# Linear attention on query features turned by VectorE instead of TensorE, with some VectorE work on GpSimd

## The chip, the cores and the metric

The kernel runs on one core of a Trainium2 chip. A core has five engines that work side by side and wait for one another through semaphores: TensorE (PE in the profile; PEld is its loading of weights), VectorE (DVE), ScalarE (ACT), GpSimd (POOL) and SyncE (SP, which here only issues DMAs). The time is that of one execution on the device, in microseconds; less is better.

## The reference

Two branches work on the same normalised tokens x (S = 2048 tokens, D = 512), and their sum and x make the output. Cut to what matters:

```python
xn = layernorm(x)
# A: linear attention, H = 32 heads of Dh = 16, features by two softmaxes
q, k, v = split(xn @ wqkv)
phi_q = concat(softmax(q @ w_phi), softmax(-(q @ w_phi)))      # 32 features a head
phi_k = concat(softmax(k @ w_phi), softmax(-(k @ w_phi)))
kv  = einsum("bhsf,bhsd->bhfd", phi_k, v);  z = sum_s phi_k
o   = (phi_q @ kv) / (phi_q @ z + 1e-6)
A   = o @ wo
# B: gated MLP with a product over tokens, Fh = 688
u   = gelu(xn @ w_in);  z1, z2 = u[:, :Fh], layernorm(u[:, Fh:])
B   = (z1 * (w_sp @ z2 + b_sp)) @ w_out
out = x + A + B
```

## The kernel before

Tokens are cut into 16 tiles of 128 rows. All large products are made from split operands: a value is rounded to a high part (`round_h`, on ACT), the rest is taken by a subtraction (`rest_l`, on VectorE unless another engine is named), and `mm3` (L55 to L57) adds three TensorE products, high by high, high by low and low by high.

The work goes in stages. First, projections: for each tile the features of q and k before their last scaling are made and those of q are stored in DRAM (`e_d`, 1024 values a token and 64 reciprocals of the softmax sums), as is `z1`; k's are added into the key-value sums. From these come `kvT` (the key-value matrix of each head, 16 x 32) and `zb` (the key sums, one row of 1024 copied to every partition). The features of q of tiles 0 and 1 are finished here already and stored back. Then the second half of `w_in`, its layer norm, and the product over tokens (`g`, L55 to L57, until about 494 us), made with seven products in place of eight in blocks of two by two; VectorE prepares its operands (`prep_a`, L537 to L541) and ACT and VectorE round them (L47, L51). The gated rows go through DRAM and come back turned (`uT`, `ut`).

The last stage makes the output, tile by tile. For a tile:

- `q_fin` (L494 to L501) finishes the q features on VectorE: weigh the 1024 features by `zb` (L494), sum them by head (L495), form the scale of each head (L496 to L499), scale the features (L501).
- `attend_T` (L896, L898) turns the features of two tiles on TensorE, sixteen transposes of 128 x 128, and ACT copies them out of PSUM (L900).
- `attend` (L912) multiplies the turned features of two tiles with `kvT`: sixteen products, each on a 64-row by 32-column part of the array, 256 columns (two tiles) long. ACT rounds the result and VectorE takes the rest (`oT`).
- `gated` joins the turned gate (L774, ACT), rounds it (`uh`, ACT) and takes the rest (`ul`, L51, VectorE).
- `project_u` multiplies it with `w_out` (17 products of 512 columns, `pout<-wu`, with L933), `project_o` adds the attention with `wo` (12 products, `pout<-woh`), VectorE adds x (`xr`, L944) and SP stores the rows.

The order on an engine is that of the program where the text puts instructions behind others with `tc.issue_after`; a planner orders the rest. In the last stage a pair of tiles goes `project_u`, `attend`, `project_u`, two `project_o`, `attend_T` of the next pair. Features are finished three tiles ahead. From tile 6 on, POOL copies finished features to another tile by a DMA (`er<-et`, L872), so that the transposes can read them in the faster type.

SP's queue is served in order: loads of `et` (from `e_d`), of `ut` and of `xr`, and the stores of the output, which wait for L944.

Of the kernel before, what the change touches and what calls it, by code (L numbers as in the profile page):

```python
# [19 lines left out]
P = 128  # L20
S, D, H, DH, FH = 2048, 512, 32, 16, 688
NT = S // P
# [17 lines left out]
def mixer(ctx: ExitStack, tc: tile.TileContext, x, x_t, wv, wqkT, phi_bd, wo, w_in, wst, b_r, w_out, out):  # L40
# [449 lines left out]
    def q_fin(et, tmp, zb):  # L490
# [3 lines left out]
        dve.tensor_tensor(tmp, e, zb, op=ALU.mult)  # L494
# [6 lines left out]
        return e, dve.tensor_tensor(heads(e), heads(e), bc(w, 2 * H), op=ALU.mult).ins  # L501
# [46 lines left out]
    with ExitStack() as p1:  # L548
# [41 lines left out]
        for s in range(NE):  # L590
            et = load_q(s, tb.tile([P, QW], F32, tag="et", bufs=2, name="et"))
            tmp = zw.tile([P, 4, FC], F32, tag="z2", bufs=2, name="qtmp").rearrange("p a b -> p (a b)")[:, :NF]
            e, _ = q_fin(et, tmp, zb)
            sp.dma_start(e_d[s, :, :NF], e)
# [131 lines left out]
    def gate(i, cb, z, planes):  # L726
# [9 lines left out]
        dve.tensor_copy(z[:, :, rm], rh.bitcast(F32))  # L736
        planes = planes.bitcast(U16).rearrange("p (k two n) -> p k two n", k=2, two=2)
        for k in range(2):
            act.activation(planes[:, k], halves(z[:, k]), AF.Copy)
# [12 lines left out]
    def split_w(t, h, l):  # L752
        return round_h(act, h, t), rest_l(l, t, h)
# [23 lines left out]
    def gate_parts(u, h, l, rt):  # L777
        full = slice(0, KF * P)
        round_h(act, h, u[:, full])
        lasts[1] = rest_l(l, u[:, full], h)  # L780
# [6 lines left out]
    def first_gate(t, rt):  # L787
        b = slot("uh_ul", F32R)
        u = xz2.tile([P, 2, 2, FC], F32, tag="b", name="u0").rearrange("p a b c -> p (a b c)")[:, :UP]
        return gate_parts(joined(t, u), b[:, :KF * P], b[:, KF * P:2 * KF * P], rt)  # L790

    lasts, wu = [None] * 6, []

    def first_q(s):
        e = slot("eq", F32R)[:, :NF]
        sp.dma_start(e.bitcast(F32), e_d[s, :, :NF])
        return e
# [12 lines left out]
    g, es, ets = {}, {}, {}  # L810
    for n in range(NC):
# [16 lines left out]
        if n == NC - 3:  # L828
            zs = slot("zb", F32R)
            zb, ident_r = zs[:, :NF].bitcast(F32), zs[:, NF:NF + P]  # L830
            round_h(act, ident_r, ident)
# [4 lines left out]
            q2 = slot("qtmp")[:, :NF]  # L836
        if n == NC - 2:
            u1t = load_u(1, slot("u1").bitcast(U16)[:, :2 * UP])
            es[0], es[1] = first_q(0), first_q(1)
            ets[3] = load_q(3, slot("et"))  # L840
            wo_raw = []
            for c in range(ND):
                rows = [(r, r + QP) for r in range((c % 2 * NG * 2 + c // 2) * QP, D, 2 * QP)][:NG]
                t = ws.tile([P, QC, P], F32, tag=f"f{c // 2}", bufs=2, name="wof").rearrange("p a b -> p (a b)")
                with tc.issue_after(load_q.last):
                    wo_raw.append(load_part((sp, pool)[c % 2], wo, rows, t))
    cb = drain(NP - 1, g, slot("c").rearrange("p (a b) -> p a b", a=4))
    with tc.issue_after(cb[1]), tc.issue_after(cb[2]):
        uT.append(first_gate(u1t, wu_rest[1]))
    with tc.issue_after(lasts[1]):  # L850
        es[2], last = q_fin(ets.pop(2), q2, zb)
    mid.close()

# [5 lines left out]
    fin = []  # L859
# [176 lines left out]
```

## Time and profile before

| what | value |
|---|---|
| median of 3 runs | 629.76 us (629.31 to 629.93) |
| profiled execution, first to last instruction | 628.4 us |
| PE busy | 622.3 us (99%) |
| VectorE busy | 505.3 us (80%) |
| ScalarE busy | 313.5 us (50%) |
| GpSimd busy | 121.0 us (19%) |
| DMA, mean over the span | 180 GB/s |

The profiled execution is one run under the profiler; the time of a run holds about 1.4 us outside this span. A busy PE is not a PE at its peak: products are pipelined, a product's row of 0.39 us stands for some 0.23 us of the chain.

Rows of a group give line, engine, operation, result and operands with their shapes, the count, then the busy time in us, the mean of one in ns, and the idle time of the engine before them with what ended it. Rows of a timeline or of the chain begin with start and duration in us. Rows of a windows view give a stretch, its length, the busy time of PE, PEld, DVE, ACT and POOL in it, the clock granted to TensorE, the share of the DMA engines and GB/s. Rows of one line's instructions give the shortest, median and longest duration in ns.

### The profile page before, as it was taken

Reading aid. Unit: us, or ns where it says so; the run is one execution under the profiler, and the core shown is the slowest. Engines: PE = TensorE matmul, PEld = TensorE weight load, DVE = VectorE, ACT = ScalarE, POOL = GpSimd, SP = SyncE. Lnnn points to the kernel's source line nnn. Section 1 sums busy time; section 2 is a strip of 40 time slices with the busy share of each in tenths; the row PEclk is TensorE's granted clock in tenths of the full one; section 3 lists DMA queues with packets and bytes.
Section 4 is the critical chain, followed back from the end, with each engine's and each line's share of the span. In section 5 each row is a group of like instructions: output and inputs, shape, how many; then the busy total and the mean of one; then the engine's idle time right before and its main releaser. Section 6 shows DMA issues by size and latency. Waiting matters only on the chain.

```text
span 628.4 us, 11487 instructions
## 1 busy us (share of the span) xinstructions
PE 622.3 (99%) x4375; PEld 563.1 (90%) x4375; DVE 505.3 (80%) x925; ACT 313.5 (50%) x463; POOL 121.0 (19%) x213
## 2 busy tenths in 40 slices
PE   9999999999999999999999999999999999999997
PEld 6888888888888999999999999999999878877776
DVE  5979989998988579989987677786777789989721
ACT  5623333432343447788553654546445655557550
POOL 4552232222101004552010110101101200110100
PEclk9999999999999999999999999999999999999999
DMA  8467767555653861001467758667588966897921
GB/s 326 152 160 163 200 176 162 166 157 151 165 164 106 265 211 68 2 1 57 138 173 186 221 176 203 202 184 226 165 197 297 287 227 230 268 278 263 293 83 35
DMA packets 67091, 112.85 MB, mean 180 GB/s; under 512 B 30588, under 2 KB 32124, under 8 KB 67036
## 3 DMA queue, kind: packets, MB, share of 16 engines
q1 hardware_dynamic: 53036, 63.35, 34.8%
q0 software_dynamic: 11408, 42.61, 23.8%
q10 hardware_dynamic: 2592, 6.16, 2.6%
q8 instruction: 34, 0.56, 0.4%
q14 instruction: 21, 0.17, 0.1%
HBM read 60.69 MB, written 31.48 MB: 147 GB/s over the span
## 4 chain that ended last, share of the span: by engine, by line
PE 96%; DVE 3%; issue 0%; ACT 0%
PE g L57 11%; PE g L56 11%; PE g L55 11%; PE proj L55 6%; PE zps L55 6%; PE proj L57 6%; PE proj L56 6%; PE zps L57 6%; PE zps L56 6%; PE pout L55 6%; PE pout L56 5%; PE pout L57 5%; PE po L912 1%; PE kvps L322 1%; PE ptq L898 1%; PE pout L933 1%
## 5 line engine op out<-in xcount | busy, mean ns | idle before, releaser
L55 PE MATMUL g<-B,A 128*128 128x344 f32 x448 | 143.2, 320 | 0.0
L56 PE MATMUL g<-B,A 128*128 128x344 f32 x448 | 143.2, 320 | 0.0
L57 PE MATMUL g<-B,A 128*128 128x344 f32 x448 | 143.0, 320 | 0.0
L57 PEld LDWEIGHTS g<-B,A 128*128 128x128 f32 x448 | 84.1, 188 | 0.2 <-DVE A L51 0.2
L56 PEld LDWEIGHTS g<-B,A 128*128 128x128 f32 x448 | 84.2, 188 | 0.0
L55 PEld LDWEIGHTS g<-B,A 128*128 128x128 f32 x448 | 84.2, 188 | 0.0
L47 ACT ACTIVATE A<-S 128x512 fp32r<-128x512 f32 x64 | 39.4, 628 | 63.3 <-DVE S L538 40.4
L116 ACT ACTIVATE e<-e,r_x 128x1024 f32<-128x1024 f32 x32 | 36.7, 1148 | 46.0 <-DVE e L115 44.1
L51 DVE TENSOR_TENSOR A<-S,A 128x512 fp32r<-128x512 f32 x64 | 43.1, 684 | 9.7 <-ACT A L47 9.6
L55 PE MATMUL proj<-wqk_h,xT 128*128 128x512 f32 x124 | 49.6, 400 | 0.0
L57 PE MATMUL proj<-wqk_h,xT 128*128 128x512 f32 x124 | 48.8, 394 | 0.0
L56 PE MATMUL proj<-wqk_l,xT 128*128 128x512 f32 x124 | 48.7, 393 | 0.0
L118 DVE TENSOR_REDUCE sm<-e 128x64 f32<-128x1024 f32 x32 | 38.6, 1210 | 9.7 <-ACT e L116 9.5
L47 ACT ACTIVATE A<-wf 128x512 fp32r<-128x512 f32 x64 | 33.0, 516 | 19.4 <-PE g L57 8.7
L51 DVE TENSOR_TENSOR A<-wf,A 128x512 fp32r<-128x512 f32 x64 | 35.2, 549 | 9.2 <-ACT A L47 9.0
L55 PE MATMUL zps<-w_h,xT 128*128 128x344 f32 x128 | 41.8, 326 | 0.4 <-ACT z1f L146 0.3
L57 PE MATMUL zps<-w_h,xT 128*128 128x344 f32 x128 | 40.9, 319 | 0.0
L56 PE MATMUL zps<-w_l,xT 128*128 128x344 f32 x128 | 40.8, 319 | 0.0
L537 DVE TENSOR_TENSOR S<-wf 128x256 f32<-128x256 f32 x32 | 13.4, 420 | 27.1 <-DMA wf<-in_wst 27.1
L146 ACT ACTIVATE z1f<-zps,r_x 128x344 f32<-128x344 f32 (+1 forms) x30 | 17.0, 565 | 33.8 <-PE zps L57 33.3
L302 ACT ACTIVATE v<-proj,r_x 128x512 f32<-128x512 f32 x16 | 11.0, 685 | 44.2 <-PE proj L57 41.7
L900 ACT ACTIVATE f<-ptq 128x512 f32<-128x512 f32 x32 | 16.5, 604 | 26.7 <-PE ptq L898 16.8
(199 smaller groups left out, 1546.4 us busy)
## 6 DMA issues: line engine op xcount, KB each, us to landing
wf<-in_wst SPq DMA_DIRECT2D x64, 256.0 KB, 3.9
e_d<-e POOLq DMA_DIRECT2D x16, 544.0 KB, 3.7
et<-e_d SPq DMA_DIRECT2D x16, 544.0 KB, 5.5
zacc<-e POOLq DMA_DIRECT2D x16, 512.0 KB, 4.9
z_d<-z1f ACTq DMA_DIRECT2D x16, 344.0 KB, 3.8
z1t<-z_d POOLq DMA_DIRECT2D x16, 344.0 KB, 5.8
u_d<-c POOLq DMA_DIRECT2D x14, 384.0 KB, 2.7
er<-et POOLq DMA_DIRECT2D x10, 512.0 KB, 4.9
```

Of the source, the lines that this page charges most:

```text
L47: return act.activation(h, src, AF.Copy).ins
L51: return (eng or dve).tensor_tensor(l, src, h.bitcast(F32), op=ALU.subtract).ins
L55: pe.matmul(dst, ah, bh, start=start, stop=False)
L56: pe.matmul(dst, ah, bl, start=False, stop=False)
L57: return pe.matmul(dst, al, bh, start=False, stop=stop).ins
L116: softmax_pair.exp = act.activation(e, e, AF.Exp, scale=scale).ins
L118: dve.tensor_reduce(sm, heads(e), axis=AX.X, op=ALU.add)
L146: z1_raw.last = act.activation(z[:, k], p, AF.Copy, scale=r_x[:, s:s + 1]).ins
L302: ins = act.activation(v[s], proj(s, wv_h, wv_l, rest_last), AF.Copy, scale=r_x[:, s:s + 1]).ins
L322: ins = pe.matmul(kv_acc[k:k + QP, m // 4], vs[:, m * QP:(m + 1) * QP], e[:, m * HP:(m + 1) * HP], start=s == 0 and m < 4, stop=s == NT - ...
L537: dve.tensor_tensor(sums[:, 0], b[:, 0], b[:, 1], op=ALU.add)
L900: attend_T.last = act.activation(f, pt.rearrange("p a k b -> p a (k b)"), AF.Copy).ins
```

## The change

Query features. `q_fin` no longer weighs; a function of its own does it, on an engine that is named, and `q_fin` ends with a transpose on VectorE in blocks of 32 x 32: within each block of 32 tokens and one head's 32 features, features come to lie on the partitions. Tiles 0 and 1 are stored turned. The transposes on TensorE, the copies out of PSUM and POOL's copies of finished features are gone.

Attention. Four copies of the key-value matrix (`kv4`), one for each 32 partitions, replace `kvT`. One run takes four token tiles: 64 products, each on a 32 x 32 part of the array and 128 columns long (32 tokens of each of four tiles); the order takes first the two upper strips of 32 rows, then the two lower ones. There are four runs instead of eight.

Engines. GpSimd takes the weighing of tiles 2 to 15, the rests of the gate for tiles 1 to 15, and the rests of `w_out` and `wo`. Two early weighings and the rest of gate 0 stay on VectorE.

Order. The last stage is written out by hand: every step stands behind the last instruction of the same engine (`in_line`). PSUM buffers for the output go from three to four, those for the rest from five to four. `wo` is loaded in four DMAs instead of sixteen.

The core of the diff:

```diff
+    def q_weigh(et, tmp, zb, eng):
+        return eng.tensor_tensor(tmp, et[:, :NF], zb, op=ALU.mult).ins
+
-    def q_fin(et, tmp, zb):
+    def q_fin(et, tmp, eT):
...
-        dve.tensor_tensor(tmp, e, zb, op=ALU.mult)
         dve.tensor_reduce(t, heads(tmp), axis=AX.X, op=ALU.add)
...
-        return e, dve.tensor_tensor(heads(e), heads(e), bc(w, 2 * H), op=ALU.mult).ins
+        dve.tensor_tensor(heads(e), heads(e), bc(w, 2 * H), op=ALU.mult)
+        return dve.transpose(eT, e).ins
...
     def split_w(t, h, l):
-        return round_h(act, h, t), rest_l(l, t, h)
+        return round_h(act, h, t), rest_l(l, t, h, pool)
...
-    def gate_parts(u, h, l, rt):
+    def gate_parts(u, h, l, rt, eng=None):
         full = slice(0, KF * P)
         round_h(act, h, u[:, full])
-        lasts[1] = rest_l(l, u[:, full], h)
+        lasts[1] = rest_l(l, u[:, full], h, eng)
...
+    def weigh(s):
+        tmps[s] = slot("qtmp")[:, :NF]
+        line["pool"] = q_weigh(ets[s], tmps[s], zb, pool)
...
+            kv4 = slot("kv4")[:, :4 * 2 * NG * QP].rearrange("p (r j b) -> p r j b", r=4, j=2 * NG)
+            for i in range(P // SQ):
+                sp.dma_start(kv4[i * SQ:(i + 1) * SQ].rearrange("p r j b -> p r (j b)"),
+                             kvT_d.rearrange("(r f) x -> f r x", f=SQ))
+            weigh(2)
...
+    with tc.issue_after(cb[1]), tc.issue_after(line["pool"]):
+        uT.append(first_gate(u1t, wu_rest[1], pool))
...
+    pso = ctx.enter_context(psum("pso", 4))
+    pst = ctx.enter_context(psum("pst", 4))
...
+    def features(s):
+        with in_line():
+            line["dve"] = q_fin(ets.pop(s), tmps.pop(s), turned(s))
...
+    def attend(k):
+        eg = egs.pop(k)
+        oT = [cw.tile([P, NG, QT, P], F32R, tag=f"oT{n}", bufs=1, name="oT") for n in "hl"]
+        po = [pst.tile([P, NG, QT, SQ], F32, tag="po", name="po") for _ in range(P // SQ)]
+        with in_line():
+            for half in range(2):
+                for g in range(NG):
+                    for a in range(2):
+                        for c in range(4):
+                            for i in (2 * half, 2 * half + 1):
+                                rows = slice(i * SQ, (i + 1) * SQ)
+                                h = 8 * g + 2 * c + a
+                                pi = pe.matmul(po[i][c * SQ:(c + 1) * SQ, g], kv4[rows, h % 4, h // 4],
+                                               eg[rows, :, h * SQ:(h + 1) * SQ], start=a == 0, stop=a == 1,
+                                               skip_group_check=True).ins
+            for i in range(P // SQ):
+                h, l = (t[:, :, :, i * SQ:(i + 1) * SQ] for t in oT)
+                ai = round_h(act, h, po[i])
+                vi = rest_l(l, po[i], h)
...
+    with in_line():
+        for c in range(ND):
+            ai, gi = split_w(wo_raw[c], wo_h[:, c], wo_l[:, c])
...
+    features(2)
+    project_u(0)
...
+    gated(2)
+    features(3)
+    project_u(1)
...
+    gated(3)
+    fetch_u(6)
+    weigh_next(4)
+    project_u(2)
+    fetch_q(5)
+    for k in range(NT // QT):
+        b = k * QT
+        oT = attend(k)
+        project_u(b + 3)
+        if k == 2:
+            with in_line():
                 gate(NP - 1, cb, z, gt.tile([P, 2 * UP], F32, tag="pl", name="pl"))
...
+        for i in range(b, b + QT):
+            last = i == b + QT - 1
+            weigh_next(i + 5)
+            fetch_q(i + 6)
+            if i + 4 < NT and i != b + 2:
+                features(i + 4 - last)
+            project_o(i, oT)
+            if last:
+                if i + 4 < NT:
+                    features(i + 4)
+                    project_u(b + 4)
+            if i + 4 < NT:
+                gated(i + 4)
+                if i + 7 < NT and i + 7 != NT - 2:
+                    fetch_u(i + 7)
+        if k < NT // QT - 1:
+            project_u(b + 5)
+            project_u(b + 6)
+        if k == 0:
+            z = load_z1(NP - 1)
```

220 lines of the change are left out of this document (76 added, 144 removed).

## The prediction

> **What bounds the kernel now.** I read the page's busy times first, then its chain, then the last stage alone, because the change sits almost entirely behind the spatial product.
>
> ```profile
> PE 622.3 (99%) x4375; PEld 563.1 (90%) x4375; DVE 505.3 (80%) x925; ACT 313.5 (50%) x463; POOL 121.0 (19%) x213
> PE 96%; DVE 3%; issue 0%; ACT 0%
> ```
>
> TensorE (PE) carries the chain from end to end. The windows view over two token-tile pairs of the last stage shows what stands beside it:
>
> ```profile
> 544.60:560.56 15.96, 15.96 (x108) 12.64 (x107) 14.89 (x22) 8.39 (x12) 2.84 (x6) 1.00 0.94 265
> 560.56:576.52 15.96, 15.96 (x108) 12.63 (x107) 13.98 (x23) 9.64 (x13) 1.06 (x2) 1.00 0.91 298
> ```
>
> A pair takes 15.96 us and PE is busy for all of it; but VectorE (the fourth figure, DVE) has 14 to 15 us of work in it, GpSimd (POOL) only 1 to 3. So PE bounds the stage with a second engine 1 to 2 us behind it: a cut on PE pays only as far as VectorE can follow. The chain in order of time, same stage, with its ends and its shares by line:
>
> ```profile
> by line: PE pout L55 23.9%; PE pout L56 22.5%; PE pout L57 22.5%; PE po L912 6.1%; PE ptq L898 5.3%; PE pout L933 5.1%; PE g L56 3.3%; PE g L57 3.3%; PE g L55 3.2%; PE ptq L896 2.4%; DVE c L712 0.4%; DVE xr L944 0.3%; issue 0.1%
> 494.54 0.59 DVE c L712
> 495.26 0.47 PE pout L55
> 544.95 1.32 PE ptq L898 x16
> 550.28 1.02 PE po L912 x32
> 551.31 0.43 PE pout L55
> 560.91 1.31 PE ptq L898 x16
> 625.06 0.42 DVE xr L944
> ```
>
> The shares are of 148.4 us (480 to the span's end). Transposes (ptq) cost 7.7% of it, 11.4 us; the attention products (po) 6.1%, 9.1 us. A pair is 1.32 of transposes, project_u of one tile, 1.02 of attention, project_u of the next, and two project_o. From 546.27 to 550.28 one project_u takes 4.0; the 15.96, less 1.32, 1.02 and twice 4.0, leaves 5.6, or 2.8 for a project_o. The stage runs from 495.26 to 625.06: 129.8 us.
>
> **The change on PE.** All ptq work goes: minus 11.4 us. Attention goes from eight runs of 16 products to four runs of 64, each of 128 columns. The order takes two of the four row strips at a time, so eight tiles are in flight, not sixteen. How fast eight tiles go, and how fast passes can start, two rows of the timeline show:
>
> ```profile
> 502.86 0.45 PE L912 MATMUL po<-f,kvT 64*32 64x256 f32 x8
> 43.22 1.10 PE L322 MATMUL kvps<-e,v 128*32 128x64 f32 x64
> ```
>
> The first is all that had started by 502.95, of 32 passes (two for each fp32 product): eight start together and the next wait for a free tile. So 1.02 us is 32 x 256 column passes on eight tiles. The new run has 128 x 128 column passes, twice as many: 2.0 us. Were it bound by starting passes at the second row's 1.10/64 = 17 ns, it would be 2.2; with sixteen tiles overlapping, 1.0. I take 2.0, since the order gives eight. Four runs: 8.0 against 9.1. PE's saving is 11.4 + 1.1 = 12.5 us if nothing else stops it. A group of four tiles then takes 2 x (15.96 - 1.32 - 1.02) + 2.0 = 29.2 us on PE, against 31.9.
>
> **The change on VectorE.** The same stage, groups by line and shape (count, busy, mean ns):
>
> ```profile
> L501 DVE TENSOR_TENSOR et<-et 128x1024 f32<-128x1024 f32 x10 | 12.2, 1224 | 0.3
> L495 DVE TENSOR_REDUCE et<-qtmp 128x64 f32<-128x1024 f32 x10 | 12.1, 1212 | 0.1
> L494 DVE TENSOR_TENSOR qtmp<-et,zb 128x1024 f32<-128x1024 f32 x9 | 11.0, 1219 | 2.4 <-DMA et<-e_d 2.4
> L51 DVE TENSOR_TENSOR ul<-uj,uh 128x640 fp32r<-128x640 f32 x8 | 6.4, 818 | 1.0 <-ACT uh L47 0.9
> L944 DVE TENSOR_TENSOR xr<-pout,xr 128x512 f32<-128x512 f32 x9 | 5.9, 674 | 0.0
> L51 DVE TENSOR_TENSOR oT<-po,oT 128x512 fp32r<-128x512 f32 x8 | 5.2, 680 | 0.0
> L498 DVE RECIPROCAL et<-et 128x32 f32<-128x32 f32 x10 | 3.5, 352 | 0.3
> L499 DVE TENSOR_TENSOR et<-et 128x64 f32<-128x64 f32 x10 | 2.2, 224 | 0.3
> L496 DVE TENSOR_TENSOR et<-et 128x64 f32<-128x64 f32 x10 | 2.2, 220 | 0.1
> L497 DVE SCALAR_TENSOR_TENSOR et<-et 128x32 f32<-128x32 f32 x10 | 1.9, 190 | 0.2
> L774 ACT ACTIVATE uj<-ut 128x1536 uint16<-128x1536 uint16 x8 | 15.0, 1955 | 0.0
> L47 ACT ACTIVATE uh<-uj 128x640 fp32r<-128x640 f32 x8 | 5.8, 730 | 0.0
> ```
>
> Per tile VectorE loses the weighing (L494, 1.22) and the gate residue (ul, 0.82) and gains the transpose of 1024 elements. Its only relative in the trace is 32 elements long:
>
> ```profile
> L279 DVE STREAM_TRANSPOSE nmT<-nm_pad x11: 145/203/213, 29.4 to 141.1; 128x32 f32<-128x32 f32 x11
> ```
>
> At the streaming rate of L495 it is 1.21 us; if the 58 ns between that row's shortest and median were the price of 32 elements, 1.9. I take 1.21, the row of its length. A tile's features then cost 1.21 + 0.22 + 0.19 + 0.35 + 0.22 + 1.22 + 1.21 = 4.6 us, and a group 4 x (4.6 + 0.68 + 0.67) = 23.9. The next run's products need the fourth tile's features, and VectorE gets its first residue of a run some 1.5 us after that run starts (half the products, then one ACT rounding). So the loop closes in 25.4 us: below PE's 29.2, with 3.8 to spare. This is without POOL.
>
> **The change on POOL, and what it does to VectorE.** POOL gains per tile a weighing of 1024 and a residue of 640, both with two SBUF operands. The trace has one such kind, at the start of the kernel, and one place where it meets VectorE:
>
> ```profile
> L51 POOL TENSOR_TENSOR w_l<-wrow,w_h x4: 1668/1680/1688, 23.6 to 29.8; 128x688 fp32r<-128x688 f32 x4
> L314 DVE TENSOR_TENSOR e<-e x16: 1207/1218/2008, 30.6 to 201.9; 128x1024 f32<-128x1024 f32 x16
> 28.24 3.30 POOL L51 TENSOR_TENSOR w_l<-wrow,w_h 128x688 fp32r<-128x688 f32 x2
> 31.49 1.55 POOL L91 TENSOR_TENSOR r_x<-mv_x,mhalf 128x1 f32<-128x1 f32 x1
> 27.63 1.20 DVE L118 TENSOR_REDUCE sm<-e 128x64 f32<-128x1024 f32 x1
> 30.61 2.01 DVE L314 TENSOR_TENSOR e<-e 128x1024 f32<-128x1024 f32 x1
> ```
>
> POOL needs 1.68 us for 688 elements, 2.44 ns each: 1.56 for a residue, 2.50 for a weighing, 1.25 for 512. L314, two SBUF operands, has a median of 1.22 in sixteen; the one issued at 30.61, under POOL's operation that ends at 31.54, is the longest, 2.01: it waited the other's end out. The reduction at 27.63, one operand, was not held. POOL's next, at 31.49, in turn waited for VectorE. So the two exclude each other when both read two SBUF tensors. POOL also gets in between two such VectorE operations:
>
> ```profile
> 264.73 0.82 DVE L51 TENSOR_TENSOR B<-z,B 128x688 fp32r<-128x688 f32 x1
> 265.47 0.51 DVE L626 TENSOR_TENSOR T<-z,T 128x344 f32<-128x344 f32 x1
> 264.86 1.12 POOL L91 TENSOR_TENSOR rstd<-mv,mhalf 128x1 f32<-128x1 f32 x1
> ```
>
> POOL's operation, issued under the first, ends at 265.98 together with L626, and not an operation's length behind it: it stepped in between. VectorE's oT and xr steps read PSUM and one SBUF tensor and are free of this; of the features L496, L497, L499 and L501 are not: a stretch of about 2.2 us per tile, reciprocal included, into which POOL can step up to four times.
>
> One group, with 0 at the run's start. ACT rounds until 3.3, joins the gate (1.95) and rounds it (0.73); POOL's residue starts near 6, just when VectorE is at L499: held 1.5, or 3.8 where the weighing behind it steps in before L501. The second tile is held 0 to 1. The second-next weighing waits for its et, whose load stands in SP's queue behind the out store, which waits for xr, and lands late:
>
> ```profile
> et<-e_d SPq DMA_DIRECT2D x8, 544.0 KB, 5.5
> ```
>
> It lands near 18, so this weighing and the residue queued behind it fall on the third tile: held 1.2 to 2.7. Then weighing, residue and weighing come back to back, 6.6 us, against the 3.1 of transpose, xr and reduction that they can hide under: held 3.5. Sum 6.2 to 11; I take 9.0 of POOL's 16.2 us per group. The group closes in 25.4 + 9.0 = 34.4 us. PE, done at 29.2, idles 5 us before each run: what is late next is VectorE.
>
> By the Trainium skill (GPSIMD Engine Reference, 3.1 Elementwise) a two-input operation costs about 2.6 cycles an element, 4.5 us for 2048; by that, as an estimate, a weighing takes 2.25 us, the wait shrinks a tenth and the time comes out near 634. The trace's 2.44 ns is a little slower than this, and I keep it.
>
> **Start and end of the stage.** PE could start the first run after three project_u, 12.0 us after 495.26. VectorE needs 2 x 4.6 = 9.2 from 495.1; POOL has at that time a weighing, four residues of wo (5.0) and three gate residues, 12.2 us nearly without a pause. If each of eight two-operand steps met one, VectorE would lose some 8 to 9; with none, 0. I take 7.3: 16.5 us. After the last run stand 2.0 + 4.0 + 4 x 2.8 = 17.2 us of PE with no features.
>
> **Edits at nothing.** Evictions of ptq on ACT, the er copies, fewer and longer wo loads, four kv4 loads instead of one: ACT has 7.6 us idle a pair, and the transfers land ahead; without that cover a late wo is worth up to its own landing, a few us. Two early transposes, 2.4 us, lie under PE's projections. Six wu residues on POOL (7.5 us) meet the preparation of the last weights, almost all of it two-operand: 0 to 2 us; I take 0.5. The last gate moves into the third group, 2.2 us of VectorE, where two weighings fall away: nothing net.
>
> **Sum.** 16.5 + 3 x 34.4 + 17.2 = 136.9 against 129.8: plus 7.1, plus 0.5, in a span of 628.4: 636.0. Runs stand at a median of 629.76, 1.4 above the span: 637.4, say 637.
>
> **Rivals.** B: POOL falls beside VectorE's one-operand steps, and PE stays the bound. For it: 16.2 us a group against 20 us of such steps; against it: the order, which releases POOL's work just ahead of L496 to L501. Then minus 12.5: 617. It decides from under 3.8 us held per group. C: held in part, 5 to 7 us a group: at 6.0 the group is 31.4, the start 14, the stage 125.4: minus 4.4, 625. Faster than before ends at about 7 us a group. D: A, and PE's idle lowers its clock. The windows row after PE's last product (625.0) has
>
> ```profile
> 626.00:628.40 2.40, 0.00 (x0) 0.00 (x0) 0.00 (x0) 0.00 (x0) 0.00 (x0) 0.97 0.16 55
> ```
>
> so the granted clock (0.97) falls within about 3 us of idling. Each run, after 5 us of idle, would go at a lower clock; were it half, 2.0 more each, 8 in four: 645. The Trainium skill (TensorE: Matmul & The Clock Gate, Part 1) has half the clock after an idle window of some 3.4 us; the row agrees that it falls, and no run here shows how long it stays down.
>
> **Chances.** A 0.45 (631 to 642), D 0.12, B 0.22 (615 to 620), C 0.21 (620 to 631). A measurement of this kernel can tell 0.2% (1.3 us) from no change. Faster by more: B, and two thirds of C, 0.36; within: 0.08; slower: 0.56. The range leaves out half of B's low end and the top of D: 616 to 645.
>
> **What would show it.** Right: no ptq rows, po runs of 128 passes near 2.0 us; L496 to L501 with maxima of 1.5 to 3 us above their minima of now; POOL near 1.6 and 2.5 us an operation; PE idle some 5 us before a run, put down to the transpose. Wrong: those rows as short as now and PE busy throughout (B); or a transpose row of 1.9 us, or POOL's residue arriving after PE's project_u, which would make the stage longer for another reason.

## The result and the profile after

The changed kernel takes 669.16 us (median of 4 runs, 667.43 to 669.63) against 629.85 us (629.31 to 630.40): 1.0617 times as long, interval 1.0602 to 1.0632. The profiled execution has a span of 667.9 us, against 628.4, so 39.5 us have to be found. The page's busy times, the clock granted to TensorE in 40 slices, and the shares of the chain by engine:

```profile
PE 637.8 (95%) x5015; PEld 579.1 (87%) x5015; DVE 532.3 (80%) x902; ACT 299.7 (45%) x430; POOL 186.4 (28%) x236
PEclk9999999999999979999999999999999897896969
PE 66%; DVE 15%; DMA 10%; issue 4%; POOL 2%; ACT 2%; SPq 0%; DVEq 0%; POOLq 0%; ACTq 0%
```

PE was busy for 622.3 us and is now busy for 637.8, though its 11.4 us of transposes are gone; the clock dips in slice 15 and in the last quarter; and 30 points of the chain have gone from PE to others. There are two places. The first lies before the last stage. The waits between 225 and 255 us, and the windows there (busy PE, PEld, DVE, ACT, POOL; clock; DMA):

```profile
ACT L661 <- DMA e_d<-qtmp: 15.9, 1, 15.9
PE zps L55 <- ACT z L661: 5.5, 1, 5.5
```

```profile
235.00:240.00 5.00, 2.02 (x13) 1.73 (x12) 4.96 (x8) 0.00 (x0) 0.00 (x0) 1.00 0.26 105
240.00:245.00 5.00, 2.50 (x9) 2.50 (x10) 2.70 (x8) 4.38 (x7) 0.96 (x3) 0.57 0.27 108
245.00:250.00 5.00, 5.00 (x26) 5.00 (x26) 4.33 (x11) 3.78 (x6) 4.39 (x10) 0.74 0.00 0
```

The early, turned features are written over `qtmp`, one of the two `z2` buffers that the second half of `w_in` needs. Before, such a buffer was free after the sum; now the store to DRAM reads it until 240.6. ACT waits for that store, PE for ACT, and the clock is at half for some time behind. The first `pout` starts at 502.4 in place of 495.3: 7.1 us.

The second is the last stage. From its first `pout` (502.4) to the end of PE's last product (664.4) it takes 162.0 us, against 129.8. Windows from the first `pout` to the first run's start, from run to run, and from the last run to the end:

```profile
502.40:522.02 19.62, 14.38 (x51) 10.41 (x51) 16.62 (x20) 10.78 (x13) 16.48 (x12) 0.91 0.87 306
522.02:558.89 36.87, 32.61 (x374) 26.46 (x374) 31.01 (x36) 13.46 (x16) 20.20 (x10) 0.94 0.53 174
558.89:600.69 41.80, 36.64 (x373) 29.94 (x374) 33.75 (x36) 13.44 (x16) 16.78 (x8) 0.83 0.47 133
600.69:640.73 40.04, 36.46 (x373) 29.90 (x374) 31.58 (x40) 17.49 (x19) 12.09 (x8) 0.84 0.37 114
640.73:667.90 27.17, 23.64 (x350) 21.21 (x350) 5.50 (x9) 2.17 (x4) 0.00 (x0) 0.81 0.12 40
```

A group was forecast at 34.4 us; it takes 36.9, 41.8 and 40.0. In the second, VectorE (fourth figure of the windows) is busy for 33.75 and idle for 8.05; forecast were 23.9 + 9.0 busy and 1.5 idle. So the busy part is right to 1 us, and VectorE's idle time is 6.5 longer. In 7.2 of the 8.05 us VectorE waits, in two pieces, for ACT to round what the run has made (total, times, longest):

```profile
DVE oT L51 <- ACT oT L47: 7.2, 2, 4.5
```

The four runs alone (busy PE with matmuls, clock, DMA):

```profile
522.02:527.51 5.49, 4.12 (x258) 0.99 0.36 140
558.89:566.54 7.65, 7.33 (x256) 0.50 0.13 40
600.69:608.25 7.56, 7.52 (x257) 0.50 0.16 39
640.73:648.07 7.34, 7.34 (x257) 0.50 0.02 4
```

2.0 us were forecast for each. Here is the first error, and it is one of counting: the loops of `attend` go over 2 halves, 4 groups, 2 heads, 4 column strips and 2 row strips, which is 128 products, not the 64 that the description of the change and the prediction give. With two passes for each fp32 product a run has 256 passes, as the rows count. At full clock the first run is 5.5 us and at half clock the others are 7.3 to 7.7. What the first one spends its time on, in three windows:

```profile
522.02:523.02 1.00, 1.00 (x73) 1.00 0.99 398
523.02:525.45 2.43, 2.43 (x193) 1.00 0.40 154
525.45:527.09 1.64, 0.27 (x17) 1.00 0.00 0
```

246 passes start in 3.43 us, 13.9 ns each; then none starts for 1.64 us, and ten more follow (the last window's 17 are passes still running, and the next's first). In that gap PE waits for nothing that the profile shows ("issue"). The DMA queues from 524 to 525 us hold a transfer of a kind of its own, one block of 0.02 MB (16 KB) of instructions, which ends at 525.7, as the gap begins:

```profile
q8 instruction: 1, 0.02, 7.8%
```

A run is 512 instructions on PE, a load and a product for each pass. Queue 8 carries PE's instructions: the pages count 34 blocks before and 39 after, and PE has 4375 and 5015 pairs of load and product, 34.2 and 39.2 times 256 instructions. The Trainium skill (Runtime: NRT & Kernel Launch, Instruction fetch mechanics) says that an engine's instructions come in 16 KiB blocks of 256, the next fetched while the current one runs, at a cost that is mostly hidden. A run spans two such blocks by this; here the gap begins as a block lands and lasts 1.64 us, so this cost is not hidden. Experiment 12 comes back to it.

VectorE and POOL from 495 us on, by line and shape (count, busy, mean ns, idle before):

```profile
L491 POOL TENSOR_TENSOR qtmp<-et,zb 128x1024 f32<-128x1024 f32 x14 | 34.0, 2430 | 12.5 <-DMA et<-e_d 12.0 <-DVE et L500 0.5
L51 POOL TENSOR_TENSOR ul<-uj,uh 128x640 fp32r<-128x640 f32 x14 | 24.6, 1760 | 32.9 <-ACT uh L47 31.0 <-issue 1.9
L503 DVE TENSOR_TENSOR et<-et 128x1024 f32<-128x1024 f32 x14 | 24.5, 1747 | 0.5
L504 DVE STREAM_TRANSPOSE eg<-et 128x1024 f32<-128x1024 f32 x14 | 17.4, 1245 | 0.6 <-DMA eg<-e_d 0.2
L501 DVE TENSOR_TENSOR et<-et 128x64 f32<-128x64 f32 x14 | 11.2, 803 | 0.5
L499 DVE SCALAR_TENSOR_TENSOR et<-et 128x32 f32<-128x32 f32 x14 | 10.8, 775 | 0.5
L498 DVE TENSOR_TENSOR et<-et 128x64 f32<-128x64 f32 x14 | 8.4, 597 | 0.5
```

L498 to L503 are the former L496 to L501. Their means were 220, 190, 224 and 1224 ns; they are 597, 775, 803 and 1747: 2.06 us longer a tile, 8.3 a group.

PE's waits over the stage:

```profile
PE po L916 <- DVE eg L504: 11.2, 3, 4.8
PE pout L57 <- POOL ul L51: 3.8, 1, 3.8
PE po L916 <- issue: 1.4, 1, 1.4
PE pout L57 <- POOL uh_ul L51: 1.0, 1, 1.0
```

PE idles 2.9, 4.8 and 3.5 us ahead of runs 2 to 4, for the transpose, and these are the runs at half clock.

### The profile page after: what moved, and what is told of

It reads as the page before. It is cut to its first block, busy times and chain, and to the rows that moved or that the text cites. A ratio compares the mean times of both kernels' runs of the same rounds, so it can differ in the third digit from the quotient of the medians.

```text
span 667.9 us, 12741 instructions
## 1 busy us (share of the span) xinstructions
PE 637.8 (95%) x5015; PEld 579.1 (87%) x5015; DVE 532.3 (80%) x902; ACT 299.7 (45%) x430; POOL 186.4 (28%) x236
## 4 chain that ended last, share of the span: by engine, by line
PE 66%; DVE 15%; DMA 10%; issue 4%; POOL 2%; ACT 2%; SPq 0%; DVEq 0%; POOLq 0%; ACTq 0%
PE g L55 8%; PE g L56 8%; PE g L57 8%; PE proj L55 6%; PE proj L57 6%; PE proj L56 6%; PE zps L55 5%; PE zps L56 5%; PE zps L57 5%; PE po L916 4%; DVE et L503 2%; DMA et<-e_d 2%; DVE et L497 2%; DMA out<-xr 1%; PE kvps L322 1%
## 5 line engine op out<-in xcount | busy, mean ns | idle before, releaser
L51 DVE TENSOR_TENSOR A<-S,A 128x512 fp32r<-128x512 f32 x64 | 45.9, 727 | 12.6 <-ACT A L47 12.4
L55 PE MATMUL zps<-w_h,xT 128*128 128x344 f32 x128 | 41.8, 326 | 0.4 <-ACT z1f L146 0.3
L916 PE MATMUL po<-eg,kv 32*32 32x128 f32 x1024 | 26.3, 379 | 12.9 <-DVE eg L504 11.2
L491 POOL TENSOR_TENSOR qtmp<-et,zb 128x1024 f32<-128x1024 f32 x14 | 34.0, 2430 | 12.5 <-DMA et<-e_d 12.0
L916 PEld LDWEIGHTS po<-eg,kv 32*32 32x32 f32 x1024 | 23.2, 143 | 16.1 <-issue 15.2
L47 ACT ACTIVATE oT<-po 128x512 fp32r<-128x512 f32 x16 | 8.7, 594 | 61.6 <-PE po L916 61.6
```

The costliest lines, as they stand in the source:

```text
L47: return act.activation(h, src, AF.Copy).ins
L51: return (eng or dve).tensor_tensor(l, src, h.bitcast(F32), op=ALU.subtract).ins
L55: pe.matmul(dst, ah, bh, start=start, stop=False)
L491: return eng.tensor_tensor(tmp, et[:, :NF], zb, op=ALU.mult).ins
L916: pi = pe.matmul(po[i][c * SQ:(c + 1) * SQ, g], kv4[rows, h % 4, h // 4], eg[rows, :, h * SQ:(h + 1) * SQ], start=a == 0, stop=a == 1, ski ...
```

## The experiments

After this profile there were four candidate causes: the early store; the shared wait of VectorE and GpSimd; the length of a run; the clock. All ratios are to the kernel before, measured beside it (629.8 to 629.9 us).

**1. A tile of its own for the early stores** (`store_own`).

```diff
-            q_fin(et, tmp, tmp)
-            sp.dma_start(e_d[s, :, :NF], tmp)
+            eT = tb.tile([P, NF], F32, tag="eT", bufs=2, name="eT")
+            q_fin(et, tmp, eT)
+            sp.dma_start(e_d[s, :, :NF], eT)
```

> The changed kernel, with the turned features of tiles 0 and 1 written to tiles of their own instead of the buffer that the layer norm needs next. Theory S (ScalarE's gelu waits for that buffer, which the store to DRAM now reads: 5.5 us of idle PE and a lowered clock behind it): the wait of ACT z for the store of e_d is gone, PE's first product of the last stage starts near 495 instead of 502.4 us, the time is 662 us. Rival (the two transposes, 2.5 us more VectorE work in that stretch, are what delays the layer norm): the wait changes its name and the gain is under 3 us, 666 or more.

Measured: 661.61 us (659.46 to 663.94), ratio 1.0504 (1.0473 to 1.0535); 7.5 us less than the change. PE's wait of 5.5 us behind `e_d<-qtmp` is gone, the product over tokens starts at 281.8 in place of 290.2, and the first `pout` at 497.2. So the early wait was this buffer. The product over tokens itself takes 214.8 us in place of 212.2, with waits of 1.1 us for ACT and 0.6 us for VectorE's rests. They lie before 340 us, and GpSimd's residues of `w_out` begin at 479; from 460 us to the end of the product PE has no wait in this trace. So these residues cost PE nothing here.

**2. The four row strips innermost** (`order16`).

```diff
-            for half in range(2):
+            for half in range(1):
...
-                            for i in (2 * half, 2 * half + 1):
+                            for i in range(4):
```

> The changed kernel, with the four row strips innermost in the attention's order, so that sixteen tiles can be in flight instead of eight. Theory L (the run of 256 passes is bound by tiles in flight): a run at the same granted clock takes half, 3.8 us instead of 7.5 at half clock, about 1.9 at full; three groups shorten by some 3.5 us each and the last run too: 656 us. Rival (bound by starting passes or loading weights, some 15 ns each): a run stays above 6 us, the time within 2 us of 669, or 1 to 2 us longer, since ScalarE can't begin on the first half early.

Measured: 659.61 us (657.76 to 661.17), ratio 1.0471 (1.0447 to 1.0494); 9.6 us less than the change. Its first run and its last:

```profile
523.15:528.44 5.29, 3.93 (x258) 1.00 0.40 161
633.18:638.84 5.66, 5.55 (x257) 0.58 0.02 6
```

At full clock the run is 5.29 us with sixteen tiles and 5.49 with eight: 246 passes start in 3.23 us in place of 3.43, and the gap is 1.6 us in both. So the number of tiles in flight, from which the prediction took its 2.0 us, matters little at full clock: twice as many tiles bring the spacing of passes from 13.9 to 13.1 ns. What sets this spacing (starting a pass, or loading its weights) was not tested. At half clock the number matters more: 128 passes start in 3.26 us with eight tiles (25.6 ns each, the second run of the changed kernel) and in 2.41 us with sixteen (18.9 ns, the second run here). Of the 9.6 us, 5.7 are in the runs (28.0 to 22.3 us). The rest was not split further; it goes with less time at half clock, some 20 us of the last stage in place of 44. The third run, with only 0.7 us of idle time ahead of it, went at full clock.

**3. All of GpSimd's new work back on VectorE** (`all_dve`).

```diff
-        line["pool"] = q_weigh(ets[s], tmps[s], zb, pool)
+        line["dve"] = q_weigh(ets[s], tmps[s], zb, dve)
...
-        return round_h(act, h, t), rest_l(l, t, h, pool)
+        return round_h(act, h, t), rest_l(l, t, h, dve)
```

and likewise the rests of the gate.

> The changed kernel, with all that the change moved to GpSimd (weighings, rests of the gate, of w_out and wo) back on VectorE. Theory P (the stretched steps of q_fin are waits for GpSimd's operations): L498, L499, L501 and L503 fall to 0.22, 0.19, 0.22 and 1.23 us each, which gives back 8.3 us per group of four tiles, and VectorE's own work grows by 4 x (1.22 + 0.82) = 8.2: the time stays near 669, 663 to 675. Rival (the stretching has another cause, DMA or the loads of et): the steps stay long, and the group grows by 8 us, 690 or more.

Measured: 665.08 us (664.60 to 667.12), ratio 1.0569 (1.0547 to 1.0592). The scaling and the last small step, shortest, median and longest:

```profile
L501 DVE TENSOR_TENSOR et<-et x14: 224/225/227, 513.7 to 632.9; 128x64 f32<-128x64 f32 x14
L503 DVE TENSOR_TENSOR et<-et x14: 1224/1225/1227, 514.0 to 633.1; 128x1024 f32<-128x1024 f32 x14
```

In the changed kernel the longest are 2441 and 3334 ns. Without GpSimd's work not one is held, so the waits were GpSimd's. But VectorE takes on 1.22 + 0.82 us a tile, 8.2 a group, just what the waits cost, and the time hardly moves: 2.06 us held for 2.04 us of work taken off. The move to GpSimd gave VectorE nothing; the three groups together are even 5.0 us shorter without it (35.7, 39.0 and 39.0 us). The first `pout` comes 3.3 us later than in the changed kernel, behind a wait of 7.5 us for an `et` (as in experiment 5), but the first run starts at 522.05, at the same time, since PE has no rest of GpSimd's to wait for.

**4. A long attention run in the kernel before** (`before_att4`): every product of attention is issued four times.

```diff
-        for j in range(2 * NG):
+        for j in [*range(2 * NG)] * 4:
```

> The kernel before, with the products of each attention run issued four times over (same result), so that a run lasts as long as one of the changed kernel, on 64x32 tiles and with no idle PE ahead of it. Eight runs of 1.0 us grow to 3.6 to 4.1. Theory C1 (PE's clock falls only when PE idles): the granted clock stays 1.00 and the time is 629.8 + 8 x 2.6 to 3.1 = 651 to 655. Theory C2 (a long run on small tiles counts as little activity): the granted clock falls to about half within or right behind a run, and the project_u behind it is slow too: 660 or more.

Measured: 657.80 us (656.72 to 658.42), ratio 1.0441 (1.0425 to 1.0457). PE from the first run to the last, in three windows:

```profile
502.80:573.50 70.70, 65.19 (x752) 1.00 0.73 253
573.50:577.00 3.50, 3.50 (x10) 0.51 0.07 16
577.00:643.50 66.50, 66.50 (x777) 1.00 0.37 114
```

Eight runs of 128 passes, 3.7 us each, go by at full clock; the one dip follows PE's idle times of 3.2 and 2.3 us. So a long run on small tiles (64 x 32 here) doesn't lower the clock. A run that is 2.6 us longer adds 8 x 2.6 = 21 of the 28 us; the rest is the idle time and the dip.

**5. The first three mends together** (`comb_dve`).

> The changed kernel with three edits of the first experiments together: a tile of its own for the stored early features, the four row strips innermost, and every weighing and rest on VectorE. If the three costs lie one behind the other on the path (theory: each is a term of the sum), they add: 669.2 - 7.5 - 9.6 - 4.1 = 648, and the groups of four tiles close in VectorE's loop of 25.4 + 4 x (1.22 + 0.82) = 33.6 us or a little more. Rival: they overlap (the clock regained by the one order is lost again when PE waits longer for a VectorE that does all the work), and the time stays at 653 to 660. A third: with all removed, the group goes down to PE's own 32.6 and the time to 640 or less.

Measured: 660.98 us (658.43 to 662.57), ratio 1.0489 (1.0468 to 1.0510). The effects don't add. The time is 1 us above the range of the second forecast, and for another reason than it gave. PE's waits at and behind the first `pout`:

```profile
PE po L917 <- DVE eg L504: 13.5, 4, 5.0
PE pout L55 <- DVE c L717: 6.7, 1, 6.7
```

The product over tokens ends at 497.5, but VectorE stands still until 502.5: its next instruction is a weighing whose `et` has not landed (6.50 us by its timeline, put down to `et<-e_d`), and the step that frees PE's buffers (`c`) is queued behind it. In the changed kernel it is GpSimd that waits for this load, with rests of the gate behind it; here the first `pout` comes at 504.3, in place of the 497.2 of experiment 1. The move to GpSimd is worth 7 us at this one place, but at the first run's start only 1.7 of them are left (520.6 against 518.9). The groups (36.9, 39.1, 39.3) close in VectorE's time: from 557.6 to 596.6 it is busy for 30.8 of 39.1 us and waits 6.4 of the rest for the run.

**6. The clock held** (`hold_clock`): 14 products of no use, 3.3 us, ahead of runs 2 to 4, into a buffer that the run then overwrites.

```diff
+            for _ in range(14 if k else 0):
+                line["pe"] = pe.matmul(po[0].rearrange("p a b c -> p (a b c)"), wo_h[:, 0, :P],
+                                       wo_h[:, 0], start=True, stop=True).ins
```

> The changed kernel with 14 products of 512 columns, of no use, on TensorE ahead of the second, third and fourth attention run (some 3.2 us at full clock, written to a buffer of the run that the run then overwrites). They fill the idle time in which PE waits for the transpose. If that idle time is what halves the clock (theory), the runs 2 to 4 go from 7.5 to 5.3 us (3 x 2.2) and the project_u behind each from 5.7 to 6.6 to 4.2 (3 x 1.5 to 2.4): 669.2 less 11 to 14 = 655 to 658, and the records show clock 1.00 through these runs. Rival: the clock falls by the run itself (its small tiles, or its 1.6 us without instructions): then runs and time stay at 7.5 and 669 to 670. A third: the filler ends after the transpose and delays the run by what it overshoots, up to 1 us a group.

Measured: 660.00 us (659.00 to 662.63), ratio 1.0472 (1.0456 to 1.0488); 9.2 us less. Runs 2 and 3 (without the added products), and the 3.41 us behind run 2:

```profile
559.70:564.87 5.17, 4.09 (x258) 1.00 0.18 54
596.37:602.41 6.04, 4.07 (x258) 1.00 0.16 46
```

```profile
565.26:568.67 3.41, 3.41 (x10) 0.50 0.02 5
```

At 1.00 runs 2 and 3 take 5.2 and 6.0 us in place of 7.65 and 7.56. So the idle time for the transpose is what halves the clock ahead of these runs. The theory held, though the gain is 2 to 5 us short of it: behind each run, which has its own gap without instructions (1.35 to 2.24 us from start to start), one interval of 3.41 us still goes at half clock, as the last row shows. The Trainium skill (TensorE: Matmul & The Clock Gate, Part 1) has the clock at half after an idle window of about 3.4 us; the interval agrees, but here gaps of 1.35 us in the middle of work were followed by one.

**7. Half the passes** (`half_passes`): every second head's products are left out, so that half of the attention is missing and a run has 128 passes.

```diff
-                    for a in range(2):
+                    for a in range(1):
...
-                                               eg[rows, :, h * SQ:(h + 1) * SQ], start=a == 0, stop=a == 1,
+                                               eg[rows, :, h * SQ:(h + 1) * SQ], start=True, stop=True,
```

> The changed kernel without the products of every second head (64 products of 128 columns a run in place of 128, so half of the attention is left out). Theory: the run's 256 passes, against the 128 that the prediction summed, are a term of the path. At half clock a run then takes 3.75 us in place of 7.5, at full clock 1.8 in place of 5.3, since the 1.6 us without instructions after 246 passes go too: four runs save 14 to 15 us, and 669.2 becomes 654 to 656. Rival: VectorE closes the group whatever the run takes, since its rests of oT start when the first half of the run is rounded; then only that half counts for the first three runs, 3 x 1.9 + 3.7 = 9, and the time is 660.

Measured: 653.44 us (647.56 to 655.01), ratio 1.0356 (1.0317 to 1.0396); 15.7 us less, within 1 us of what the theory gave. The runs take 2.06, 3.44, 3.55 and 2.89 us, and none has a gap. The first one, at full clock, is the run that the prediction summed: 128 passes in 2.06 us, where it said 2.0. So the length of a run is on the path in full, VectorE's loop included, since VectorE's first rest of a run waits for the run.

**8. The weighing on GpSimd, alone, in the kernel before** (`before_wpool`, tiles 3 to 15).

```diff
-        dve.tensor_tensor(tmp, e, zb, op=ALU.mult)
+        (eng or dve).tensor_tensor(tmp, e, zb, op=ALU.mult)
...
-            es[s], ins = q_fin(ets.pop(s), slot("qtmp")[:, :NF], zb)
+            es[s], ins = q_fin(ets.pop(s), slot("qtmp")[:, :NF], zb, pool)
```

> The kernel before, with one part of the change alone: the weighing of tiles 3 to 15 on GpSimd. It tells whether the shared wait costs anything where VectorE is not last. Theory: L496 to L501 show maxima of 2 to 3 us (one weighing of 2.43 us each time it steps in), about 1 to 2 us held a tile against 1.22 us taken off VectorE, and the stage, which PE bounds, stays: 628.4 to 631.4 us. Rival: the cover is too thin (VectorE has 14 to 15 us of work in a pair's 15.96): the weighing takes twice as long on GpSimd and the features come late, so each pair grows by 1 to 2 us, 6 pairs, and the time is 636 to 642.

Measured: 645.93 us (643.89 to 648.25), ratio 1.0257 (1.0237 to 1.0277). The theory was wrong, and the rival's 636 to 642 was still too low. The features' steps from 503 to 572 us, and PE's longest wait:

```profile
L496 DVE TENSOR_TENSOR et<-et x10: 211/226/2432, 507.1 to 565.2; 128x64 f32<-128x64 f32 x10
L499 DVE TENSOR_TENSOR et<-et x10: 224/224/2414, 507.9 to 568.3; 128x64 f32<-128x64 f32 x10
L501 DVE TENSOR_TENSOR et<-et x10: 1214/1225/3449, 510.3 to 568.6; 128x1024 f32<-128x1024 f32 x10
```

```profile
PE pout L57 <- DVE oT L51: 10.2, 3, 6.5
```

The medians are as before; the longest are 2.2 us above them, about one weighing (2.53 us here, in the mean). By the means (0.91, 0.66 and 1.66 us) these three steps are held 1.6 us a tile, against 1.22 taken off, and the gate's rest, 1.34 us in the mean until 584, another 0.5. The chain of waits, which was PE alone from 503 on, is VectorE's until 571, and there alone 18 us are lost (the fifth run starts at 584.3 in place of 566.2); then the pairs take 15.96 us again. In a stage where VectorE has 14 to 15 us of work in 15.96, taking 1.22 us off it and letting GpSimd in made it the bound.

**9. No work for GpSimd from tile 4 on** (`no_pool_work`): the weighing is left out, and the rounded gate stands in place of its rest, so that PE's work stays and VectorE takes on nothing.

```diff
-            with in_line():
-                weigh(s)
+            tmps[s] = ets[s][:, :NF]
...
-            nxt[i] = gate_parts(u, wk.tile([P, KF * P], F32R, tag="uh", bufs=3, name="uh"),
-                                wk.tile([P, KF * P], F32R, tag="ul", bufs=3, name="ul"),
-                                wk.tile([2 * REM, P], F32R, tag="rt", bufs=3, name="rt"), pool)
+            nxt[i] = gate_parts(u, wk.tile([P, KF * P], F32R, tag="uh", bufs=3, name="uh"), None,
+                                wk.tile([2 * REM, P], F32R, tag="rt", bufs=3, name="rt"))
```

> The changed kernel without GpSimd's steps of the last stage from tile 4 on: the weighings of tiles 4 to 15 and the rests of the gate of tiles 2 to 15 are left out (sums are formed over unweighed features, and the rounded gate stands in place of its rest in the third product, so that TensorE's work stays as it is). Nothing holds L498 to L503 then, and VectorE takes on nothing. Theory (the shared wait of 8.3 us a group is on the path): the groups of 36.9, 41.8 and 40.0 us go down to TensorE's own 32.6 to 33, 20 us in three; with no idle time ahead of the runs the clock stays, 3 to 4 us behind the last run's start; and 1 to 2 at the start: 669.2 - 25 = 644. Rival (the runs and the clock are the path, and the wait on GpSimd lies beside them): as when its work went back to VectorE, 4 to 8 us: 661 to 665.

Measured: 649.38 us (645.56 to 650.64), ratio 1.0322 (1.0305 to 1.0340); 19.8 us less, between the theory's 644 and the rival's 661. The profiled execution is the shortest of the five (645.6). Windows from run to run, PE's waits, and the end of the first run:

```profile
517.37:553.79 36.42, 32.27 (x372) 26.26 (x372) 23.38 (x36) 14.03 (x18) 0.00 (x0) 0.95 0.79 269
553.79:589.58 35.79, 33.56 (x374) 27.23 (x373) 23.48 (x36) 13.38 (x16) 0.00 (x0) 0.90 0.40 116
589.58:620.17 30.59, 30.59 (x374) 25.25 (x373) 25.54 (x40) 17.53 (x19) 1.09 (x2) 1.00 0.40 121
```

```profile
PE po L917 <- issue: 7.2, 3, 4.1
PE pout L55 <- ACT uh L47: 3.0, 1, 3.0
```

```profile
525.19 0.67 PE L917 MATMUL po<-eg,kv 32*32 32x128 f32 x11 [4.14 <-issue]
```

VectorE is at 23.4 us in the first two groups: the prediction's 23.9, measured. PE no longer waits for the transpose, and the first run starts 4.65 us earlier. What is left on PE is one wait for ACT, its gaps without instructions, now up to 4.1 us, in three of the four runs, and 10 us at half clock. The third group has none of this: 30.6 us, all of it work. That is PE's own price of four tiles, against 31.9 before (and 29.2 forecast with half the passes); the change does take 1.3 us a group off PE, where nothing else stops it.

**10. The same with the mends of 1 and 2** (`floor`).

> The same with two edits more: a tile of its own for the early stores, and the four row strips innermost. What is left is TensorE's work and whatever else this order costs. If the early wait, the wait on GpSimd and the clock are all there was beside the longer runs: 644 - 7.5 = 636 to 637, above the 629.9 of the kernel before, so the change saves TensorE nothing even with GpSimd's work for free. Rival: 631 or less, if runs at full clock and without gaps take 3.4 us. A third: 645 and more, if a wait that no run has shown takes over (features' loads, ACT's roundings of the run).

Measured: 647.02 us (643.12 to 648.18), ratio 1.0263 (1.0230 to 1.0296). It missed the 636 to 637; the third case, 645 and more, is what came. After the start (first `pout` at 499.2) the same gaps are 8.0 us in three runs, and one wait for ACT's rounding of the gate is 4.7. So even without GpSimd's work from tile 4 on, this order stays 2.6% slower than the kernel before.

**11. The whole change with three mends** (`best_mix`: 1, 2 and 6).

> The whole change with three mends: a tile of its own for the early stores (-7.5 by itself), 14 products of no use ahead of runs 2 to 4 (-9.2 by itself), row strips innermost (-9.6 by itself, by the clock too). Theory: the first and the second add, since they act in different stages, the third adds 0 to 2 once the clock is held: 650.5 to 652.5. Rival: they overlap as in the combination with all work on VectorE (-8.2 in place of -21): 657 to 660.

Measured: 657.41 us (653.12 to 659.07), ratio 1.0428 (1.0391 to 1.0466): the rival's 657 to 660, not the sum. The first `pout` is at 497.6, but a group still waits for VectorE, so that what PE gains in a run it waits for elsewhere: gaps of 1.3 to 3.1 us for POOL's rests, for `xr` and for the transpose.

**12. A run cut in two** (`split_run`: 1 and 6, and the first six products of `project_u` between the two halves of a run).

```diff
+            if half == 0:
+                between()
...
-        oT = attend(k)
-        project_u(b + 3)
+        oT = attend(k, lambda: project_u(b + 3, 0))
+        project_u(b + 3, 1)
```

> The whole change with a tile of its own for the early stores, the 14 products ahead of runs 2 to 4, and each run cut in two halves of 128 passes with the first six products of project_u between them. Theory (TensorE runs out of fetched instructions after some 246 passes without a pause): no half shows the gap of 1.4 to 1.9 us, the halves take 1.8 us each, and the time is 1.6 us a run, 6.5 in all, under the same kernel with an uncut run (650.5 to 652.5): 644 to 646. Rival: the gap moves (into the products between, or into the second half), 651. A third: the second half's result comes 1.4 us later to VectorE, which closes the group: 653 to 656.

Measured: 658.61 us (655.01 to 660.68), ratio 1.0452 (1.0413 to 1.0491). The first half, the products between, the second half; and PE's waits in the stage:

```profile
521.34:523.10 1.76, 1.76 (x129) 1.00 0.22 87
523.10:524.88 1.78, 1.78 (x25) 1.00 0.03 9
524.88:526.91 2.03, 2.03 (x130) 1.00 0.00 0
```

```profile
PE pout L55 <- DVE xr L956: 6.7, 3, 2.6
PE pout L57 <- POOL ul L51: 3.8, 1, 3.8
```

No run of the four has a gap; in the kernels with all work every uncut run at full clock has one, of 1.35 to 2.25 us from start to start. So the gaps come from 512 instructions in some 3.5 us without a pause. The traces tie them to the transfers of instructions. Over all kernels here, the profile has 23 gaps in a run that it puts down to nothing. Their idle time is 0.5 to 4.1 us, but the next product always starts 1.24 to 1.58 us after a 16 KB block has landed on queue 8. In the changed kernel's first run that block lands at 525.72 and products start again at 527.08; in `no_pool_work` the block lands at 523.7, 2.7 us into the gap, and products start again at 525.19. So PE stands until a block of its instructions is in. Why the block comes late, and later in some runs than in others, is not shown.

The time is above all three forecasts, and within the intervals that of `best_mix` (which has the strips innermost besides, so the two are not a strict pair). PE waits 4.0 us for VectorE ahead of the first `pout`, and 6.7 us for the `xr` steps that free its output buffers. The three groups take 114.4 us, in `best_mix` 114.7: what PE no longer loses in its runs it waits for VectorE.

No version beat the kernel before.

## Why the prediction was wrong

It forecast a slower kernel, at 637, and 669.2 came. The wait that it forecast was there and had the forecast size; most of the excess came from a term that it had sized wrong by a count, the attention run. By its own steps, in the profiled execution:

| step | forecast us | measured us | excess |
|---|---|---|---|
| early transposes and residues, up to the first `pout` | 0.5 | 7.1 | 6.6 |
| first `pout` to first run | 16.5 | 19.6 | 3.1 |
| three groups | 103.2 | 118.7 | 15.5 |
| last run's start to PE's end | 17.2 | 23.7 | 6.5 |

The four excesses sum to 31.7, and 636.0 + 31.7 = 667.7, within 0.2 of the span.

**The attention run failed, and it carries most.** The "four runs of 64, each of 128 columns" are four of 128, and "I take 2.0" came of it: four runs take 28.0 us, not 8.0. Of these 20 us, some 14 are the run at full clock (5.5 in place of 2.0), and some 6 the clock. The size for the passes that it did count was right: `half_passes` has the run as forecast, at 2.06. For 256 passes it would have given 4.0, where 3.4 and a gap of 1.64 us came; the gap stood in no step. "1.0 with sixteen tiles overlapping" would not have come: in `order16` passes start every 13 ns at full clock, against 14 with eight tiles.

The run enters the groups through VectorE. The prediction gave VectorE 1.5 us from the run's start to its first rest ("half the products, then one ACT rounding"); in the second group it waits 4.5 us for the first half and 2.7 for the second.

**"Two early transposes, 2.4 us, lie under PE's projections" failed.** Not their 2.4 us mattered but where their result lay. The prediction asked what hides the instructions and not who needs their buffer next; the store holds a `z2` buffer, and it cost 7.1 us (`store_own`: 7.5).

**The shared wait was right, in size and effect.** Forecast 9.0 us a group (6.2 to 11), measured 8.3; maxima of 1.5 to 3 us above the minima, measured 2.1 to 2.2 on three of the four lines (1.2 on L498); POOL's weighing forecast at 2.50 and measured at 2.43, its residue at 1.56 and 1.76 (1.56 where nothing held it). Its placement within a group was not followed tile by tile. `all_dve` took every wait away; `no_pool_work` took 19.8 us of time away, of which 4 to 5 lie ahead of the first run. The rule that the two engines hold each other out, and for a whole instruction, is stated by the Trainium skill (SBUF — State Buffer, section SBUF: two separate sides); L503's longest, 3334 against 1224 ns, agrees.

**The clock was a rival at 0.12 and was part of the main case.** Rival D gave 2.0 us a run at half clock, on a run of 2.0; runs 2 to 4 lost 1.9 to 2.2 us each, and `project_u` behind runs 1 to 3 takes 5.6 to 6.4 us in place of 4.05. Once A holds, PE idles ahead of each run, and the condition of D is met: D should have been a term of A, not a case beside it. `hold_clock` puts it at 9.2 us.

**B and C were not near.** Even with GpSimd's work left out from tile 4 on the time is 649. B's 617 rested on minus 12.5 us of PE; a group without a gap gives 1.3 us, so four would give some 5 (an estimate from that group).

**The transpose** was put at 1.21 us and takes 1.245. **The start** was forecast at VectorE's pace, but PE goes into the first run without waiting for the features. It had a wait that the prediction named as a sign of being wrong: POOL's residue comes after PE's `project_u`, 3.8 and 1.0 us of PE's idle time, and 3.4 us at half clock behind the longer one. **The six residues of `w_out`**, put at 0.5 us, cost nothing: the product over tokens takes 212.2 us, as before.

## What to carry to other kernels

Count a loop nest twice, once from the loops and once from what the operation has to do, before a duration is multiplied by it: the largest error here was a factor of two in a count. When a result goes to a new buffer, ask who needs that buffer next and what holds it until when; a hidden instruction can leave a store that is not hidden. Before work is moved from VectorE to GpSimd, ask which of VectorE's operations with two SBUF operands it will meet: here 2.04 us of work taken off a tile came back as 2.06 us of waiting, and in a kernel where VectorE was second by 1 to 2 us, the weighing alone cost 16 us.

## What the runs showed of the hardware

- In 23 runs of 512 instructions PE stops for 0.5 to 4.1 us, and it starts again 1.24 to 1.58 us after a 16 KB block of instructions has landed, in every one of them. It doesn't stop in 256 instructions at a time with 1.8 us of long products between, nor in 256 in 3.7 us (`before_att4`). The place differs (after 128 to 255 passes), and the third runs of `no_pool_work` and `floor` went through the same 512 instructions at full clock without a stop, so where a block begins may count.
- fp32 passes of 128 columns on 32 x 32 tiles start 13.9 ns apart at full clock with eight tiles in flight and 13.1 with sixteen; at half clock 25.6 with eight and 18.9 with sixteen.
- Stretches at half clock last 3.41, 6.83, 10.24 or 13.65 us here, one to four times 3.41. They follow idle times of 1.35 to 5 us, though not each of them (1.6 us in the third run of `order16` passed without). In the changed kernel a run of 7.5 us at half clock didn't bring the clock back, though PE was busy throughout; it came back some 5 us into the long products behind. With sixteen tiles in flight (`order16`, fourth run) it came back within the run, after 4.8 us.
- A transpose of 128 x 1024 fp32 elements in 32 x 32 blocks takes 1.245 us on VectorE, as long as an operation of two operands on as many (1.225).
